# Softmax attention with a feed-forward branch on one core: another order of work in the opening and around five groups of pair sums

## The chip, the cores and the metric

The kernel runs on one core of a Trainium2 chip. The core has five engines that work side by side, each through its own list of instructions in order: TensorE (PE, matrix products), ScalarE (ACT, here mostly exponentials), VectorE (DVE), GpSimd (POOL) and SyncE (SP, which only issues transfers). They wait for one another through semaphores. Products land in PSUM, which has eight banks of 128 partitions x 512 float32; all else that is on the chip lies in SBUF. The metric is the device time of one execution in microseconds (us). The kernel before takes 664.33 us, the median of three runs (664.21 to 664.44).

## The reference

Input x has 2048 rows of 640. Attention has 32 heads of 20 columns and one key and value head for all of them. Two branches work on the same normalized rows and are added to x:

```
xn = layernorm(x)
q = (xn @ wq).reshape(2048, 32, 20);  k = xn @ wk;  v = xn @ wv
p = softmax(q @ k.T * 20**-0.5)              # 32 heads x 2048 x 2048
attn = (p @ v).reshape(2048, 640) @ wo
ffn = relu(xn @ w1 + b1)**2 @ w2 + b2        # 1536 hidden columns
out = x + attn + ffn
```

Most of the time goes into the 32 x 2048 x 2048 exponentials.

## The kernel before, in words

**Tiles.** A score tile is 128 keys x 512 queries of one head. A block is four heads and one of four chunks of 512 queries; there are 32 blocks and 16 key tiles, so 512 units of four tiles each. PE makes a tile by one product of 20 rows (kT times qT) into a PSUM bank; seven banks are shared by such tiles and other work, and the eighth collects probabilities times values of the current block.

**Two ways through the exponential.** 348 units go to ACT: the line L1328 takes two score tiles (128x1024) from two banks, writes their exponentials into two of 16 slots of the buffer PT, and PE multiplies them by the values (vx). The order of these exponentials is fixed. The other 164 units, called sets here, go past ACT. DVE evicts each of the four tiles of such a set in a scaled and shifted 16-bit integer form whose bits, read as bf16, stand near an exponential (L1551). Three copies of the set follow, each with another constant added to the integers: POOL makes most (L1571, or two copies by one instruction, L2121, a joint pass), DVE some (L1572). The four terms, summed with weights, come near the exponential. PE multiplies each term by the values (vx for two terms, vxs, the values with a weight, for the others).

**Pair sums.** Two terms with one weight can be added first, so that PE has one product less for each of four heads. For this POOL issues a transfer within SBUF that adds one term into the other (tx<-tx, L1588; both pairs of a set at once, L2119; L2047 is the same where it was put in later), or DVE adds them (L1593, L2048). The product of the summed term waits for the landing. Each term lies in one of 15 buffers (tx); a buffer is used anew when all that reads it is done. A sum overwrites its second term, so the first sum of a set must come behind a joint pass that reads that term.

**Opening.** Rows of x come in by eight transfers. For each of the first four tiles of 128 rows DVE or ACT makes the statistics, DVE the normalized rows (L822), PE five transposes (T0 to T3, L866), ACT or DVE the eviction (L871 on ACT), then PE the key rows (K0 to K3), the query rows of the first block (Q0_0 to Q0_3) and the values (V0_0 to V0_3). ACT evicts the four query pieces (L887) and then begins with the first exponential. Ahead of the transposes PE runs dummy products of a constant tile of ones (`ones`, L734, in buffer OR) with a tile of zeros (`zero`, L735): three at L861 and 15 at L905. They compute nothing that is used.

**What sets the order.** A planner inside the program walks through a model of the engines while the kernel is built: each step carries a modelled duration, a priority and due times, and tables of rules change them by stage. Then a table (PLAN) permutes each engine's list, and a second model (replay) settles the places of the buffers. So an instruction's place does not stand in the code by its line. L729 is a helper that records nearly all products, so its line says nothing of which product it is; the names of the tiles do.

Of the kernel before, what the change touches and what calls it, by code (L numbers as in the profile page):

```python
# [2257 lines left out]
```

## Time and profile before

| what | before |
|---|---|
| time, median of 3 runs | 664.33 us (664.21 to 664.44) |
| span of the profiled execution | 663.4 us |
| ACT busy | 649.3 us (98%), of it 640.3 us in 696 exponentials |
| PE busy | 655.2 us (99%), with modelled ends |
| DVE busy | 627.1 us (95%) |
| POOL busy | 533.1 us (80%) |
| joint passes on POOL (L2121) / single passes (L1571) | 16 / 369 |
| transfers that add a pair (512 KB) | 111, landing after 5.7 us (median) |

The profile gives no device time for the profiled execution alone, only its span, from its first instruction to its last; the median of the runs lies 0.9 us above that span. In the profile's rows a group has a count, the busy time in us, the mean length of one in ns, and the idle time ahead of it with the engine that ended it. Engines start an instruction before the last one has ended, so the busy time of a group is less than count times mean. PSUM buffers are called ps in the rows; PT, tx, kT and qT are as above, xnT is the transposed normalized rows, and names of form in_A_x_dram are inputs.

### The profile page before, as it was taken

Reading aid. Unit: us, or ns where it says so; the run is one execution under the profiler, and the core shown is the slowest. Engines: PE = TensorE matmul, PEld = TensorE weight load, DVE = VectorE, ACT = ScalarE, POOL = GpSimd, SP = SyncE. Lnnn points to the kernel's source line nnn. Section 1 sums busy time; section 2 is a strip of 40 time slices with the busy share of each in tenths; the row PEclk is TensorE's granted clock in tenths of the full one; section 3 lists DMA queues with packets and bytes.
Section 4 is the critical chain, followed back from the end, with each engine's and each line's share of the span. In section 5 each row is a group of like instructions: output and inputs, shape, how many; then the busy total and the mean of one; then the engine's idle time right before and its main releaser. Section 6 shows DMA issues by size and latency. Waiting matters only on the chain. (4 is left out here: it accounts for less than half of the span.)

```text
span 663.4 us, 22377 instructions
## 1 busy us (share of the span) xinstructions
PE 655.2 (99%) x9569; PEld 211.9 (32%) x9570; DVE 627.1 (95%) x1125; ACT 649.3 (98%) x719; POOL 533.1 (80%) x528
## 2 busy tenths in 40 slices
PE   8999999999999999999999999999999999999997
PEld 4432222332322223323332222333333322223444
DVE  8979999999999999999999999999999999999997
ACT  7999999999999999999999999999999999999995
POOL 1629899898998889898999988889899999799300
PEclk9999999999999999999999999999999999999999
DMA  8594957788997995696957645798788655858741
GB/s 289 160 241 109 197 119 161 163 183 189 190 191 162 185 179 117 127 182 125 181 105 154 126 91 102 154 180 176 151 170 167 131 126 97 172 104 182 136 111 70
DMA packets 53528, 102.09 MB, mean 154 GB/s; under 512 B 15916, under 2 KB 31164, under 8 KB 53364
## 3 DMA queue, kind: packets, MB, share of 16 engines
q0 software_dynamic: 18544, 68.17, 55.5%
q1 hardware_dynamic: 34164, 31.94, 16.6%
q8 instruction: 75, 1.23, 0.8%
q10 hardware_dynamic: 720, 0.54, 0.3%
q14 instruction: 25, 0.20, 0.1%
HBM read 23.26 MB, written 10.01 MB: 50 GB/s over the span
## 5 line engine op out<-in xcount | busy, mean ns | idle before, releaser
L1328 ACT ACTIVATE PT<-ps 128x1024 bf16<-128x1024 f32 x696 | 640.3, 1121 | 2.2 <-PE ps L729 1.7
L1551 DVE TENSOR_SCALAR tx<-ps 128x512 uint16<-128x512 f32 x656 | 424.0, 683 | 21.1 <-PE ps L729 14.2
L1571 POOL INT64_ADD tx<-tx x369 | 391.2, 1130 | 57.3 <-PE ps L729 16.8
L729 PE MATMUL ps<-qT,kT 20*128 20x512 bf16 x2048 | 262.9, 384 | 0.3
L729 PEld LDWEIGHTS ps<-qT,kT 20*128 20x128 bf16 x2048 | 67.3, 91 | 253.3 <-ACT PT L1328 132.9
L729 PE MATMUL ps<-PT,vx 128*32 128x512 bf16 x1392 | 131.3, 384 | 0.0
L729 PE MATMUL ps<-tx,vxs 128*32 128x512 bf16 x1220 | 112.9, 384 | 0.4 <-DMA tx<-tx 0.3
L1588 POOL DMA_DIRECT2D tx<-tx x103 | 102.8, 998 | 7.7 <-POOL tx L1571 6.9
L729 PE MATMUL ps<-w_sb,big 128*32 128x320 bf16 x1536 | 82.6, 302 | 0.0
L729 PE MATMUL ps<-tx,vx 128*32 128x512 bf16 x864 | 81.0, 384 | 1.6 <-DMA tx<-tx 1.6
L729 PE MATMUL ps<-xnT,w_sb 128*32 128x512 bf16 x960 | 78.9, 383 | 0.0
L1572 DVE TENSOR_SCALAR tx<-tx 128x2048 uint16<-128x2048 uint16 x91 | 63.3, 707 | 0.8 <-DMA tx<-tx 0.5
L729 PEld LDWEIGHTS ps<-PT,vx 128*32 128x32 bf16 x1392 | 34.3, 94 | 39.7 <-issue 35.2
L729 PEld LDWEIGHTS ps<-w_sb,big 128*32 128x32 bf16 x1536 | 34.0, 95 | 31.1 <-issue 20.3
L729 PEld LDWEIGHTS ps<-tx,vxs 128*32 128x32 bf16 x1220 | 28.5, 94 | 36.5 <-issue 27.6
L1054 DVE TENSOR_SCALAR hT_tmp<-ps,b1col 128x512 bf16<-128x512 f32 x48 | 35.7, 743 | 1.6 <-PE ps L729 1.3
L729 PE MATMUL ps<-xnT,wq_sb 128*32 128x512 bf16 (+2 forms) x480 | 35.6, 356 | 0.0
L729 PE MATMUL ps<-wo_c,OC 128*32 128x320 bf16 x576 | 31.8, 301 | 0.0
L2121 POOL INT64_ADD tx<-tx x16 | 30.6, 1913 | 0.5
L729 PEld LDWEIGHTS ps<-tx,vx 128*32 128x32 bf16 x864 | 20.9, 95 | 27.9 <-issue 20.5
L729 PEld LDWEIGHTS ps<-xnT,w_sb 128*32 128x32 bf16 x960 | 19.3, 94 | 25.7 <-issue 17.4
L1416 DVE COPY OR<-ps 128x512 f32<-128x512 f32 x30 | 20.5, 682 | 0.9 <-PE ps L729 0.6
(91 smaller groups left out, 242.6 us busy)
## 6 DMA issues: line engine op xcount, KB each, us to landing
tx<-tx POOLq DMA_DIRECT2D x111, 512.0 KB, 5.7
tx<-tx POOLq DMA_DIRECT2D x7, 1024.0 KB, 9.0
w_sb<-in_B_w_dram SPq DMA_DIRECT2D x8, 480.0 KB, 9.4
big<-OR SPq DMA_DIRECT2D x71, 40.0 KB
xb<-in_A_x_dram SPq DMA_DIRECT2D x1, 2560.0 KB, 12.2
xb<-b2r POOLq DMA_DIRECT2D x1, 2560.0 KB, 19.0
xr<-xb SPq DMA_DIRECT2D x16, 160.0 KB, 3.4
out_dram<-out_sb SPq DMA_DIRECT2D x15, 160.0 KB, 2.9
```

Source lines behind the costliest of these rows:

```text
L729: return lambda e: e.matmul(out_(), l, val(r), start=val(start), stop=val(stop), tile_position=tp, skip_group_check=loose)
L1054: o = Op(f"RL{qc}_{f}", "DVE", 0.66, [lambda e: e.tensor_scalar(out=hT_tmp[:, k % 2, :], in0=ps[:, at(bk), :], scalar1=b1col[:, f:f + 1], ...
L1328: o = Op(f"ACT{st_['j']}", "ACT", ACB + ACM * n, [lambda e: e.activation(out=PT[:, slots[0].n:slots[0].n + n, :], in_=src(), func=AF.Exp, ...
L1416: tn = op(f"TN{b}", "DVE", 0.60, lambda e: e.tensor_copy(out=OR[:, a, :], in_=ps[:, PVB, :]), [lastpv] + or_users[a], prio=0)
L1551: d1 = op(f"D1_{n}_{i}", "DVE", 0.60, lambda e: e.tensor_scalar(out=L()[:, cs].bitcast(U16), in0=ps[:, ref.n, :], scalar1=XA, scalar2=XB, ...
L1571: fns = dict(POOL=lambda e, T=T, j=j: e.int64_add(out=T().bitcast(I64), in0=L().bitcast(I64), in1=TSTEP * j * 0x0001000100010001), DVE=lam ...
L1572: DVE=lambda e, T=T, j=j: e.tensor_scalar(out=T().bitcast(U16), in0=L().bitcast(U16), scalar1=TSTEP * j, scalar2=None, op0=ALU.add))
L1588: p = op(f"AD{a}_{n}", "POOL", ADDUR, lambda e, src=src, dst=dst: e.dma_start(dst(), src(), accum_op=ALU.add), dp + [ad_last.get(k)], dma= ...
L2121: fn = lambda e, x=x: e.int64_add(out=two(*sorted((x["ref"][2].n, x["ref"][3].n))).bitcast(I64), in0=two(*sorted((x["ref"][0].n, x["ref"][ ...
```

## The change

The planner, its rules and the replay are taken out, and the order is written down: a table ORDER has the names of all steps of each engine in their order, with the banks or buffers that they take; TENANTS says which terms live in each of the 15 tx buffers, one behind the other; HELD says behind which DVE step a POOL step has to wait. The functions that make the steps are the same. Cut to its core:

```diff
-RULES = {0: {'WARM': 1},
...
-PLAN = {
-    "PE": (
-        "0*39 1 2 16 21 4 0 28 1*2 2 0 15 ...
...
+NSET = 15
...
+ORDER = {
+    "PE": (
+        "W4 W5 W6 warm: warm: warm: warm: warm: warm: warm: warm:S1a warm:S1b warm:S1b warm:AG1 warm:S3a warm:S3a T0 T1 T2 T3 K0 Q0_1 Q0_0 Q0_3 Q0_2 K1 K2 q:0,1,2@0,1,2 q:3,4@3,4 V0_0 V0_1 "
...
+TENANTS = (
+    ("108 119 172 246 319 298 368 446 426 507 ...
...
+        for e in ENG:
+            nth = {}
+            for word in ORDER[e].split():
...
+                if k in ("fill", "warm"):
...
+                else:
+                    nth[k] = nth.get(k, -1) + 1
+                    o = made[k if k in made else f"{k}.{nth[k]}"]
+                    o.banks = ns
+                    names[e].append(o.name)
```

Compared step by step, the order differs in five stretches, in the time of the kernel before: from the start to some 74 us (called A below), 147 to 168 us (B), 231 to 247 us (C), 280 to 301 us (D) and 452 to 494 us (E). Everywhere else each engine has the same steps one behind the other. Over the whole, 13 dummy products stand where 15 stood (the three ahead of them stay), two fills of zeros instead of 12, 693 exponentials instead of 696 (six in the opening take three tiles, 128x1536), 650 evictions of scores into sets instead of 656 (six take two tiles), 86 passes on DVE instead of 91, 360 single passes on POOL instead of 369, and 23 joint ones instead of 16.

The first place is the head of DVE's list. In both, L734 (now L603) is the tile of ones, hT_tmp the zeros, and PT, ident the steps that make the identity matrix for the transposes. Before:

```order
L734 MEMSET OR 128x128
L735 MEMSET hT_tmp 128x256
L736 MEMSET scr 128x4
L738 MEMSET PT 128x1
L739 MEMSET ident 128x64
L741 TENSOR_SCALAR PT<-PT 128x1
```

and now:

```order
L607 MEMSET PT 128x1
L610 TENSOR_SCALAR PT<-PT 128x1
L610 TENSOR_SCALAR PT<-PT 128x2
L610 TENSOR_SCALAR PT<-PT 128x4
L604 MEMSET hT_tmp 128x256
L610 TENSOR_SCALAR PT<-PT 128x8
L610 TENSOR_SCALAR PT<-PT 128x16
L611 STREAM_TRANSPOSE PT<-PT 128x32
L608 MEMSET ident 128x64
L612 TENSOR_SCALAR ident<-PT 32x32
L614 MEMSET vx 128x16
L616 MEMSET zeros 128x16
L605 MEMSET scr 128x4
L612 TENSOR_SCALAR ident<-PT 32x32
L615 MEMSET vx 128x16x11
L603 MEMSET OR 128x128
L612 TENSOR_SCALAR ident<-PT 32x32 x2
```

The tile of ones, which the first product of PE reads, has gone from the first to the sixteenth place of DVE's list; the steps ahead of it are the same ones as before, in another order.

The second place is the head of PE's list, up to the first scores (ps<-qT,kT). L861 and L905, now L709 and L1029, are the dummies; wk_c is K, wq_sb is Q0, wv_c is V0. Before:

```order
L861 MATMUL ps<-hT_tmp,OR 128x512 x3
L905 MATMUL ps<-hT_tmp,OR 128x512 x15
L866 MATMUL ps<-ident,big 128x128 x20
L729 MATMUL ps<-xnT,wk_c 20x128 x20
L729 MATMUL ps<-xnT,wq_sb 20x128 x60
L729 MATMUL ps<-xnT,wk_c 20x128 x20
L729 MATMUL ps<-xnT,wq_sb 20x128 x20
L729 MATMUL ps<-xnT,wk_c 20x128 x20
L890 MATMUL ps<-wv_c,xnT 128x20 x10
L729 MATMUL ps<-xnT,wk_c 20x128 x20
L729 MATMUL ps<-qT,kT 128x512 x4
```

and now:

```order
L709 MATMUL ps<-hT_tmp,OR 128x512 x3
L1029 MATMUL ps<-hT_tmp,OR 128x512 x13
L699 MATMUL ps<-ident,big 128x128 x20
L599 MATMUL ps<-xnT,wk_c 20x128 x20
L599 MATMUL ps<-xnT,wq_sb 20x128 x80
L599 MATMUL ps<-xnT,wk_c 20x128 x40
L599 MATMUL ps<-qT,kT 128x512 x5
L702 MATMUL ps<-wv_c,xnT 128x20 x10
L599 MATMUL ps<-xnT,wk_c 20x128 x20
```

All four query pieces now stand ahead of the second key tile, and the first five score tiles ahead of the values and the last key tile; the transposes stay behind all dummies.

The third place is POOL's list in stretch B, around the sets 106 to 109. L1571 (now L1094) is a single pass, L1588 (now L1118) the issue of a pair sum, L1100 a joint pass. Before:

```order
L1588 DMA tx<-tx 128x2048
L1571 ISA tx<-tx 128x1024 x5
L1588 DMA tx<-tx 128x2048
L1571 ISA tx<-tx 128x1024 x2
L1588 DMA tx<-tx 128x2048
```

and now:

```order
L1118 DMA tx<-tx 128x2048
L1100 ISA tx<-tx 128x2x1024
L1094 ISA tx<-tx 128x1024 x3
L1118 DMA tx<-tx 128x2048
L1100 ISA tx<-tx 128x2x1024
L1118 DMA tx<-tx 128x2048
L1094 ISA tx<-tx 128x1024 x3
```

The first three issues in each are the sums of the sets 108, 107 and 106, one behind the other. Ahead of set 107's stand one joint pass (set 109, copies 2 and 3) and three single ones instead of five; between set 107's and set 106's one joint pass (set 106) instead of two single ones.

Besides these, SP's loads stand in another order (the first part of wq behind the rows 8 to 11, the rest of wq behind b1), ACT issues wk behind its table load and wv behind the statistics, and POOL issues the transfer that adds b2 to x (xb<-b2r, L1153) behind its last normalized rows, just ahead of the library load that its passes need, instead of four rows earlier.

More of the change, by code (lines that the diff above doesn't have):

```diff
@@ new lines, in transposes, with v_mats @@
+        def transposes(st, bk):
+            return [(lambda e, dt=dt: e.transpose(out=psbf(bk)[:, dt * 128:(dt + 1) * 128], in_=xn_sb[:, st, dt:D:DT], identity=ident[:])) for dt in range(DT)]
+        def v_mats(st, bk):
+            return [(lambda e, dt=dt: e.matmul(ps[:, at(bk), DH * (st % 4):DH * (st % 4) + DH], xnT[:, dt, st * 128:(st + 1) * 128], wv_c[:, dt, :], start=(dt == 0), stop=(dt == DT - 1)))
+                    for dt in range(DT)]
+        VB0, WB = SHARED[2], 7
+        k_of, q_of, v_of, vs_of, first_rel = {}, {b: [] for b in range(NBLK)}, {}, {}, {}
@@ L907, in need_te, with evac @@
+        def evac(ref, *args, **kw):
+            o = op(*args, **kw)
+            o.gives = [ref]
+            return o
         def need_te(sts):
             return [te_op[st] for st in sts]
[L910 to L921 removed]
@@ new lines, in bass_parallel_sum__grouped_kv_mqa__dense_activation_squared_relu__prompt_kernel @@
+        for b in range(NBLK):
+            pv_all[b][-1].ends[1] = True
+            made[f"TN{b}"].deps += pv_all[b]
+        seq = {e: [made[w] for w in names[e]] for e in ENG}
+        assert sum(map(len, seq.values())) == len(made), [w for w in made if w not in sum(names.values(), [])]
+        for o in made.values():
+            o.deps = [made[d] if isinstance(d, str) else d for d in o.deps]
+        same = {}
+        for o in made.values():
+            if o.dma is not None:
+                same.setdefault((id(o.dma), o.tgt[1]), []).append(o)
@@ new lines, in bass_parallel_sum__grouped_kv_mqa__dense_activation_squared_relu__prompt_kernel @@
+        slot_rel = {}
+        pv_tile = {HPG * o.unit + h: o for l in pv_all for o in l if o.unit is not None for h in range(HPG)}
+        for o in seq["ACT"]:
+            for n, t in zip(o.slots, o.tiles):
+                if n in slot_rel:
+                    o.deps.append(slot_rel[n])
+                slot_rel[n] = pv_tile[t]
+        made[f"OFe{ST - 1}_0"].deps += [slot_rel[n] for n in (0, 1)]
+        made[f"OFe{ST - 1}_1"].deps += [slot_rel[n] for n in (0, 1)]
+        filler = {(u, j): o for e in ("DVE", "POOL") for o in seq[e] for u, j in o.fills}
@@ new lines, in bass_parallel_sum__grouped_kv_mqa__dense_activation_squared_relu__prompt_kernel @@
+        for n, tenants in enumerate(TENANTS):
+            free_after = list(xn_op.values()) if n >= NMORE else []
+            for k in map(int, tenants.split()):
+                u, j = divmod(k, NTERM)
+                assert sets[u].at[j] == n
+                filler.pop((u, j)).deps += free_after
+                free_after = sets[u].reads[j]
+        assert not filler
+        held = iter(HELD.split())
+        for o in seq["POOL"]:
+            if o.lock:
+                w = next(held)
+                if w != "-":
+                    o.deps.append(made[w])
```

1988 lines of the change are left out of this document (406 added, 1582 removed), and 444 rows, old and new, of tables (HELD, ORDER, PLAN, TENANTS).

## The prediction

> **What bounds the kernel now.** I read the page first, then the ACT rows of the timeline, then the waits.
>
> ```profile
> span 663.4 us, 22377 instructions
> PE 655.2 (99%) x9569; PEld 211.9 (32%) x9570; DVE 627.1 (95%) x1125; ACT 649.3 (98%) x719; POOL 533.1 (80%) x528
> L1328 ACT ACTIVATE PT<-ps 128x1024 bf16<-128x1024 f32 x696 | 640.3, 1121 | 2.2 <-PE ps L729 1.7
> ```
>
> Three engines read 95% or more, and PE's ends are modelled, so shares don't decide. The timeline of ACT from 11 us on does:
>
> ```profile
> 12.18 152.27 ACT L1328 ACTIVATE PT<-ps 128x1024 bf16<-128x1024 f32 x165 [0.23 <-PE ps L729]
> 165.09 299.03 ACT L1328 ACTIVATE PT<-ps 128x1024 bf16<-128x1024 f32 x325 [0.64 <-PE ps L729]
> 464.60 36.87 ACT L1328 ACTIVATE PT<-ps 128x1024 bf16<-128x1024 f32 x40 [0.48 <-PE ps L729]
> ...
> 556.93 97.55 ACT L1328 ACTIVATE PT<-ps 128x1024 bf16<-128x1024 f32 x106 [0.18 <-PE ps L729]
> ```
>
> From 12.18 us to 556.93 + 97.55 = 654.48 us ACT does exponentials with hardly a pause, so the span has three parts: the start of the first exponential, 696 pitches (the time from one start to the next), and a tail of 663.4 - 654.5 = 8.9 us whose order is unchanged. The span shrinks only by an earlier start, fewer exponentials, or shorter pitches. Hidden stalls lie inside the busy time, since each exponential starts before the last has ended; they show as a longer pitch. The groups by stretch give it as (busy + idle - mean) / (count - 1):
>
> ```profile
> L1328 ACT ACTIVATE PT<-ps 128x1024 bf16<-128x1024 f32 x23 | 21.4, 1038 | 0.3 <-PE ps L729 0.2
> L1328 ACT ACTIVATE PT<-ps 128x1024 bf16<-128x1024 f32 x45 | 41.7, 1086 | 0.2
> L1328 ACT ACTIVATE PT<-ps 128x1024 bf16<-128x1024 f32 x80 | 73.5, 1165 | 0.0
> L1328 ACT ACTIVATE PT<-ps 128x1024 bf16<-128x1024 f32 x24 | 22.5, 1111 | 0.6 <-PE ps L729 0.6
> L1328 ACT ACTIVATE PT<-ps 128x1024 bf16<-128x1024 f32 x19 | 17.9, 1115 | 0.0
> L1328 ACT ACTIVATE PT<-ps 128x1024 bf16<-128x1024 f32 x24 | 22.3, 1051 | 0.0
> L1328 ACT ACTIVATE PT<-ps 128x1024 bf16<-128x1024 f32 x47 | 43.5, 1084 | 0.5 <-PE ps L729 0.5
> ```
>
> These are 12 to 33 us and 33 to 74 (A), 74 to 146.6 (unchanged order, my yardstick), then B, C, D and E. The yardstick's pitch is (73.5 - 1.165) / 79 = 0.916 us. A's two halves have 0.926 (the start's wait left out) and 0.928, B 0.956, C 0.932, D 0.924, E 0.933. Above the yardstick that is 22 x 0.010 + 44 x 0.012 = 0.75 us in A, and 23 x 0.040 = 0.93, 18 x 0.017 = 0.30, 23 x 0.008 = 0.19, 46 x 0.017 = 0.80 in B to E, together 2.2. The excess is what an altered order can give back there.
>
> What stands behind it in B to E, from the waits and PE's timeline:
>
> ```profile
> PE ps L729 <- DMA tx<-tx: 1.9, 4, 0.6
> 164.29 0.40 PE L729 MATMUL ps<-tx,vx 128*32 128x512 bf16 x4 [0.64 <-DMA tx<-tx]
> 239.71 0.40 PE L729 MATMUL ps<-tx,vx 128*32 128x512 bf16 x4 [0.31 <-DMA tx<-tx]
> 292.17 0.40 PE L729 MATMUL ps<-tx,vxs 128*32 128x512 bf16 x4 [0.31 <-DMA tx<-tx]
> 463.80 0.40 PE L729 MATMUL ps<-tx,vx 128*32 128x512 bf16 x4 [0.62 <-DMA tx<-tx]
> ```
>
> PE stands still four times in the whole program for a pair sum that has not landed, once in each of B to E. Its list is in order, so the score products behind wait too, and the exponential that needs them: ACT's 0.64 at 165.09 and 0.48 at 464.60 follow.
>
> **Part 1, the start of the exponentials: +0.4 us.** The first product of PE reads the tile of ones.
>
> ```profile
> 0.82 0.17 DVE L734 MEMSET OR<- 128x128 bf16 x1 [0.82 <-PEq L2243]
> 2.58 0.97 DVE L743 TENSOR_SCALAR ident<-PT 32x32 bf16<-32x32 f32 x4
> 3.94 0.49 DVE L806 BATCH_NORM_STATS2 OR<-tx 128x6 f32<-128x320 bf16 x1
> 1.32 1.46 PE L861 MATMUL ps<-hT_tmp,OR 128*128 128x512 bf16 x3 [1.32 <-DVE PT L738]
> 7.58 1.44 PE L866 MATMUL ps<-ident,big 128*128 128x128 bf16 x20
> L905 PE MATMUL ps<-hT_tmp,OR x9: 464/631/631, 2.6 to 6.0; 128*128 128x512 bf16 x9
> L905 PE MATMUL ps<-hT_tmp,OR x8: 379/379/631, 5.6 to 7.4; 128*128 128x512 bf16 x8
> ```
>
> All constants are made when the first statistics begin at 3.94 us. With `ones` in sixteenth place the two last comparisons (2 x 0.24) stand behind it, so it is done by about 3.4 and PE begins 2.1 us later than at 1.32. The last two rows (queried before and after 6.1 us) show the dummies' durations fall from 631 to 379 ns near 6 us. Their pitch up to there is 3.4 / 8 = 0.43 us; behind it 0.24, from the weight loads of the same group, six in 1.2 us. The summary row reads "PEclk 9" for this time, so I take the change from the durations. The same sum for before: (6.15 - 1.32) / 0.43 = 11.2 dummies at 0.43 us, 6.8 at 0.24, an end at 7.8 where the transposes began at 7.58. For after, if the speed changes at the same time: 6.4 at 0.43, 9.6 at 0.24, an end at 8.45, less the same 0.2: 8.25, or 0.7 us late. Two dummies fewer save 2 x 0.24 of what would have been 1.2.
>
> Not all of it reaches the first exponential. Ahead of it ACT waited 0.23 us (above) and 0.28:
>
> ```profile
> 10.86 0.28 ACT L887 ACTIVATE qT<-ps 128x128 bf16<-128x128 f32 x1 [0.28 <-PE ps L729]
> 9.97 0.61 ACT L887 ACTIVATE qT<-ps 128x128 bf16<-128x128 f32 x3
> 9.23 1.01 PE L729 MATMUL ps<-xnT,wq_sb 128*20 128x128 bf16 x60
> 11.74 0.39 PE L729 MATMUL ps<-qT,kT 20*128 20x512 bf16 x4
> ```
>
> The fourth query piece now stands ahead of K1, the scores ahead of V0 and K3. If both waits vanish, 0.7 - 0.5 = +0.2 is left, if none, +0.7; I take +0.4. The floor is 0, because ACT's own chain behind the transposes keeps its rows; the ceiling comes with rival 1.
>
> The moved loads I cost at nothing: the first part of wq is issued two transfers later, but its first product stands at 9.23 us and moves back with the transposes; if it lands late all the same, the ceiling below holds that too. The rest of wq is needed only by block 1. POOL's moved transfer puts off the library load behind it:
>
> ```profile
> 28.58 1.81 POOL L1153 DMA_DIRECT2D xb<-b2r  x1
> 47.03 1.04 POOL L1571 INT64_ADD tx<-tx  x1 [12.09 <-PE ps L729]
> 48.71 3.07 POOL L1571 INT64_ADD tx<-tx  x3 [0.63 <-DVE tx L1551]
> 52.83 2.05 POOL L1571 INT64_ADD tx<-tx  x2 [1.06 <-DVE big L1062]
> ```
>
> The 12.09 us ahead of POOL's first pass is mostly that load. It moves by up to 1.8; the waits of 0.63 and 1.06 behind it cover 1.7, and DVE has passes there too. Uncovered, it would cost the first sets a product, a few tenths.
>
> **Part 2, three exponentials fewer: -0.2 us.** Nine pairs of tiles become six triples. The trace has no triple. Three query evictions of 128 columns, in the row at 9.97 above, have a pitch of (0.61 - 0.28) / 2 = 0.165 us; a line through that and the pairs' 0.916 gives 0.06 us for an instruction without columns, and 0.165 itself bounds it from above. Three instructions fewer save 0.18 to 0.5, or nothing where a triple waits for its third bank. I take 0.2, by the nearer rows.
>
> **Part 3, pitches in A: -0.3 us.** The bounds are 0 and 0.75. Ten fills of zeros (four products each) leave PE,
>
> ```profile
> L729 PE MATMUL ps<-kT,zeros 128*32 128x512 bf16 x48 | 4.5, 382 | 0.0
> ```
>
> and 40 of these 48 at that group's rate are 3.8 us of PE, most of it beside ACT. I take less than half of the bound, since A's pitch never held ACT for long.
>
> **Part 4, B to E: -1.6 us.** In B the late sum is that of set 106:
>
> ```profile
> 153.10 0.90 POOL L1588 DMA_DIRECT2D tx<-tx  x1
> 154.03 1.05 POOL L1571 INT64_ADD tx<-tx  x1
> 155.77 1.04 POOL L1571 INT64_ADD tx<-tx  x1 [0.68 <-DVE OC L1452]
> 156.75 0.86 POOL L1588 DMA_DIRECT2D tx<-tx  x1
> L2121 POOL INT64_ADD tx<-tx x16 | 30.6, 1913 | 0.5
> ```
>
> Before, two passes and 0.68 of waiting lie between the two issues. After, one joint pass (1.91, from L2121) does: the issue of 106 comes at about 153.10 - 0.2 (one joint and three single passes ahead instead of five single) + 0.9 + 1.95 = 155.75, 1.0 us earlier. The wait was 0.64, so the product finds its sum, if the transfer takes no longer. C to E have the same kind of edit around waits of 0.31, 0.31 and 0.62. The bounds are 0 (or a loss, rival 2) and the 2.2 us of excess; the four waits are 1.9. I take 1.6, allowing that one short wait stays. Six fewer evictions and five fewer passes on DVE lie beside ACT's work: nothing.
>
> **The sum.** +0.4 - 0.2 - 0.3 - 1.6 = -1.7 us. The page's span of 663.4 becomes 661.7; the median lies 0.9 above the span, so 664.3 becomes 662.6 us. The bounds' ends are -3.45 (0, -0.5, -0.75, -2.2) and, with rival 1's start, +2.1.
>
> **Rivals.** Rival 1: the change of the dummies' speed comes later, because PE starts later. If it depends on how long PE has been busy, the 4.8 us between 1.32 and 6.15 repeat from 3.4, and it comes at 8.2. The 16 dummies then take 11.2 pitches of 0.43 us and 4.8 of 0.24, to 9.35, less 0.2: transposes at 9.15, 1.6 late; if it comes later still, all 16 take 0.43, to 10.2, 2.4 late. So 1.6 to 2.4, about 2.0 for the first exponential less a few tenths of the vanished waits: +1.7 for +0.4, and 662.6 becomes 663.9. For it: the row of 631 ns lasts as far as 6 us and nothing in this trace shows why it ends there. Against it: if a fixed beat sets it, 2.7 us of work up to 6.15 may be enough. The Trainium skill ("TensorE: Matmul & The Clock Gate", Part 1) says that the clock opens after a busy window of about 3.4 us which runs freely and does not start with the kernel, and that the point varies from run to run. By that rule the later start risks a whole window more, and the time would scatter; the trace, with one opening near 6 us, agrees but can't show the phase. Chance 0.25.
>
> Rival 2, slower: the joint passes make new late sums. A joint pass takes 1.91 where a single copy takes 1.05, and the set's first sum must stand behind it. Where the product has less than 0.9 us of margin, PE waits as it did at 164.29. Four waits of 0.64 with none of the old excess regained give +0.4 - 0.2 - 0.3 + 2.6 = +2.5: 666.8. It decides from about 0.5 us per stretch on. For it: four late sums among 111 show margins near nothing. Against it: in B the issue comes earlier by its rows. Chance 0.11.
>
> Rival 3: the regained waits come back one product later, since the excess pitch is a shortage of PE or DVE in these stretches and not the sum's lateness; only the opening changes, -0.1 or so: 664.2. For it: C and D show excess without any idle time of ACT. Against it: E's and B's excess is about as large as their waits on PE. Chance 0.14.
>
> **How the numbers follow.** The forecast, 662.6 us, has 0.50; its own range is 661.3 to 663.7. Faster or slower by over 0.2% (1.3 us, about what a measurement of this kernel can tell from no change) means under 663.0 or over 665.7. Of the forecast 0.41 lies below 663.0 and 0.09 above; of rival 1, 0.04 below and 0.21 between; rival 3 is the same; rival 2 is slower. So faster 0.45, same 0.44, slower 0.11. The range of 8 in 10 reaches from 661.2 to 665.2: it holds the forecast's range and rivals 1 and 3, and leaves out rival 2.
>
> **What would show it.** Part 1: the first dummy near 3.4 us, the first transpose near 8.25 and the first exponential near 12.6 in ACT's timeline; a first transpose after 9 us is rival 1. Part 2: a triple with a pitch under 1.37 (one and a half pairs). Parts 3 and 4: pitches in B to E near 0.916 (0.93 leaves half), and no PE wait on tx<-tx above 0.3 us; several waits of 0.6 are rival 2, no waits but unchanged pitches rival 3. The forecast is wrong if the exponentials begin after 13.5 us, or if the stretch from the first to the last of them is not shorter by 1.5 us or more.

## The result, and the profile after

The changed kernel takes 672.0 us, the median of four runs (668.92 to 676.69), against 664.38 us before (664.21 to 665.63): 1.0114 times the time before, 95% interval 1.0078 to 1.0149. It is slower by 1.1%, and its runs scatter over 8 us where those before scatter over 1.4. Six more runs of it gave 667.97 to 677.60. The granted clock belongs to the result: it reads under 0.999 in nine of these ten runs, down to 0.984, while of 112 runs of the kernel before, timed beside the experiments, seven did so, none under 0.995. Here and below a ratio and its interval leave out single runs that lie more than 1.5% above the fastest of their kernel; the ranges in brackets hold them.

First the span and the row of the exponentials from the page of the profiled execution, and the exponentials on ACT down to their last pause of over 0.2 us (start, time from there to the next pause, the first instruction's form, the count, and in brackets the wait ahead). L1071 is what L1328 was, L599 what L729 was.

```profile
span 669.3 us, 22210 instructions
L1071 ACT ACTIVATE PT<-ps 128x1024 bf16<-128x1024 f32 (+1 forms) x693 | 640.3, 1123 | 6.9 <-PE ps L599 6.4
12.45 72.39 ACT L1071 ACTIVATE PT<-ps 128x1536 bf16<-128x1536 f32 x76
85.81 85.73 ACT L1071 ACTIVATE PT<-ps 128x1024 bf16<-128x1024 f32 x93 [0.97 <-PE ps L599]
173.11 1.02 ACT L1071 ACTIVATE PT<-ps 128x1024 bf16<-128x1024 f32 x1 [1.57 <-PE ps L599]
175.08 1.02 ACT L1071 ACTIVATE PT<-ps 128x1024 bf16<-128x1024 f32 x1 [0.95 <-PE ps L599]
176.56 1.02 ACT L1071 ACTIVATE PT<-ps 128x1024 bf16<-128x1024 f32 x1 [0.46 <-PE ps L599]
177.79 67.02 ACT L1071 ACTIVATE PT<-ps 128x1024 bf16<-128x1024 f32 x73 [0.21 <-PE ps L599]
246.29 70.01 ACT L1071 ACTIVATE PT<-ps 128x1024 bf16<-128x1024 f32 x76 [1.48 <-PE ps L599]
316.75 189.98 ACT L1071 ACTIVATE PT<-ps 128x1024 bf16<-128x1024 f32 x206 [0.46 <-PE ps L599]
```

The pauses of 0.64 and 0.48 us at 165 and 464 us have gone. In their place stand 0.97 at 85 us, 3.2 in four pieces at 172 to 178, 1.48 at 246 and 0.46 at 316. ACT's list has the same order in both kernels, so the start of one and the same exponential can be subtracted. The difference, after less before, at exponentials named by their start in the kernel before:

| start before (us) | 12.2 | 23.3 | 83.5 | 101.9 | 157.0 | 168.7 | 179.7 | 240.1 | 246.0 | 301.4 | 312.5 | 644.1 |
|---|---|---|---|---|---|---|---|---|---|---|---|---|
| after less before (us) | +0.27 | -0.07 | -0.69 | +0.54 | +0.71 | -0.17 | +3.55 | +3.64 | +4.96 | +4.58 | +5.20 | +5.23 |

The opening gains 0.96 us from the first exponential to 83 us, B 0.88 up to 169 us; between 84 and 102, 169 and 180, 240 and 246 and 301 and 312 us the kernel gives back 1.23, 3.72, 1.32 and 0.62. From 312 us on the sum does not change. Stretch E brought nothing in the end, though the wait for its pair sum has gone: the exponentials gain 0.64 us there (from +5.40 at 460 us to +4.76 at 465) and have lost it again by 490 (+5.39). PE waits for an eviction instead:

```profile
471.87 0.39 PE L599 MATMUL ps<-qT,kT 20*128 20x512 bf16 x4 [0.38 <-DVE tx L1081]
```

The rest of the 5.9 us of span, 0.7, lies behind the last exponential.

What PE, and in one case DVE, waited for at these four places, as the timelines of the two engines show it:

```profile
84.83 0.40 PE L599 MATMUL ps<-tx,vx 128*32 128x512 bf16 x4 [1.05 <-DMA tx<-tx]
170.68 0.69 DVE L971 TENSOR_TENSOR OC<-cmore 128x512 bf16<-128x512 f32 x1 [2.52 <-DMA cmore<-drs]
172.03 0.38 PE L599 MATMUL ps<-qT,kT 20*128 20x512 bf16 x1 [1.65 <-DVE tx L1081]
245.31 0.40 PE L599 MATMUL ps<-tx,vx 128*32 128x512 bf16 x4 [1.58 <-DMA tx<-tx]
315.78 0.62 PE L599 MATMUL ps<-tx,vx 128*32 128x512 bf16 x8 [0.54 <-DMA tx<-tx]
```

Three are pair sums. The one at 172 us, the dearest, goes back to another transfer: the reciprocals of the softmax sums, sent through DRAM and spread over the rows (cmore<-drs), for which the product L971 on DVE (CM0_2) waits. DVE stood still for 2.52 us, so the eviction behind it came late, so PE stood still for 1.65 us for the bank.

Then the clock closed. The windows view of PE (window, its length, busy time, instructions, the granted clock, DMA share, GB/s):

```profile
167.00:170.50 3.50, 3.38 (x59) 1.00 0.85 187
170.50:173.90 3.40, 1.87 (x21) 0.98 0.82 198
173.90:177.30 3.40, 3.40 (x31) 0.52 0.64 146
177.30:180.70 3.40, 3.40 (x53) 1.00 0.68 137
```

In the 3.4 us behind the standstill PE ran at half its clock and got 31 instructions through, against 53 in the next 3.4 us; that is where the waits of 0.95 and 0.46 come from.

How long the transfer took, by SP's timeline. Issued first are the reciprocals (drs<-R, called RS4), then, when they have landed, the two transfers that bring them back (cmore<-drs, BC4_0 and BC4_3). Before:

```profile
152.79 0.63 SPq L1423 DMA_DIRECT2D drs<-R  x1
157.77 1.42 SPq L1445 DMA_DIRECT2D cmore<-drs  x2
159.23 0.85 SPq L1420 DMA_DIRECT2D R<-drs  x1
```

and after:

```profile
153.00 0.57 SPq L943 DMA_DIRECT2D drs<-R  x1
160.95 0.77 SPq L964 DMA_DIRECT2D cmore<-drs  x1
163.00 0.87 SPq L941 DMA_DIRECT2D R<-drs  x1
163.91 0.62 SPq L964 DMA_DIRECT2D cmore<-drs  x1
```

Two things are late: the way out, from the issue of RS4 to that of BC4_0, took 7.95 us instead of 4.98, and BC4_3 now stands behind a load of x (XR2) and R<-drs (SL5) on SP's list, 2.96 us behind BC4_0, where it followed BC4_0 directly.

### The profile page after: what moved, and what is told of

Its sections match the earlier page's. It is cut to its first block, busy times and chain, and to the rows that moved or that the text cites. A ratio compares the mean times of both kernels' runs of the same rounds, so it can differ in the third digit from the quotient of the medians.

```text
span 669.3 us, 22210 instructions
## 1 busy us (share of the span) xinstructions
PE 655.2 (98%) x9525; PEld 212.7 (32%) x9526; DVE 622.9 (93%) x1114; ACT 649.2 (97%) x716; POOL 536.5 (80%) x526
## 3 DMA queue, kind: packets, MB, share of 16 engines
q8 instruction: 75, 1.23, 0.8%
## 4 chain that ended last, share of the span: by engine, by line
PE 81%; DMA 7%; POOL 6%; ACT 2%; DVE 1%; issue 1%; SPq 0%; POOLq 0%
PE ps L599 80%; DMA tx<-tx 5%; POOL tx L1094 4%; ACT PT L1071 2%; POOL tx L1118 1%; DMA drs<-R 1%; DMA cmore<-drs 1%; POOL tx L1100 1%; DVE tx L1081 1%; PE ps L1029 1%; PE ps L699 0%; PE ps L709 0%; SPq L868 0%; PE ps L702 0%; DVE PT L1007 0%
## 5 line engine op out<-in xcount | busy, mean ns | idle before, releaser
L1071 ACT ACTIVATE PT<-ps 128x1024 bf16<-128x1024 f32 (+1 forms) x693 | 640.3, 1123 | 6.9 <-PE ps L599 6.4
L1081 DVE TENSOR_SCALAR tx<-ps 128x512 uint16<-128x512 f32 (+1 forms) x650 | 423.5, 688 | 27.6 <-PE ps L599 21.0
L1094 POOL INT64_ADD tx<-tx x360 | 384.6, 1163 | 56.9 <-DVE tx L1095 23.8
L599 PE MATMUL ps<-qT,kT 20*128 20x512 bf16 x2048 | 266.2, 385 | 3.1 <-DVE tx L1081 2.0
L599 PEld LDWEIGHTS ps<-qT,kT 20*128 20x128 bf16 x2048 | 68.4, 91 | 255.6 <-ACT PT L1071 133.7
L599 PE MATMUL ps<-PT,vx 128*32 128x512 bf16 x1392 | 131.8, 386 | 0.0
L1118 POOL DMA_DIRECT2D tx<-tx x118 | 120.3, 1032 | 10.9 <-POOL tx L1094 6.9
L599 PE MATMUL ps<-tx,vxs 128*32 128x512 bf16 x1220 | 112.4, 385 | 0.0
L599 PE MATMUL ps<-tx,vx 128*32 128x512 bf16 x864 | 81.5, 385 | 3.2 <-DMA tx<-tx 3.2
L599 PE MATMUL ps<-w_sb,big 128*32 128x320 bf16 x1536 | 80.3, 302 | 0.0
L599 PE MATMUL ps<-xnT,w_sb 128*32 128x512 bf16 x960 | 78.1, 383 | 0.0
L1095 DVE TENSOR_SCALAR tx<-tx 128x2048 uint16<-128x2048 uint16 x86 | 60.0, 712 | 0.2
L599 PEld LDWEIGHTS ps<-PT,vx 128*32 128x32 bf16 x1392 | 34.3, 94 | 42.0 <-issue 36.5
L1100 POOL INT64_ADD tx<-tx x23 | 45.2, 1966 | 1.5 <-DVE tx L1095 0.8
L599 PEld LDWEIGHTS ps<-w_sb,big 128*32 128x32 bf16 x1536 | 33.6, 95 | 30.0 <-issue 19.6
L599 PEld LDWEIGHTS ps<-tx,vxs 128*32 128x32 bf16 x1220 | 28.3, 94 | 34.6 <-issue 27.5
L827 DVE TENSOR_SCALAR hT_tmp<-ps,b1col 128x512 bf16<-128x512 f32 x48 | 35.6, 742 | 2.4 <-PE ps L599 2.1
L599 PE MATMUL ps<-xnT,wq_sb 128*32 128x512 bf16 (+2 forms) x480 | 34.4, 356 | 0.0
L599 PE MATMUL ps<-wo_c,OC 128*32 128x320 bf16 x576 | 31.5, 301 | 0.0
L599 PEld LDWEIGHTS ps<-tx,vx 128*32 128x32 bf16 x864 | 20.9, 95 | 29.9 <-issue 20.7
L599 PEld LDWEIGHTS ps<-xnT,w_sb 128*32 128x32 bf16 x960 | 19.0, 94 | 26.8 <-issue 18.6
L939 DVE COPY OR<-ps 128x512 f32<-128x512 f32 x30 | 20.5, 683 | 0.8 <-PE ps L599 0.5
```

Source lines behind the costliest of these rows:

```text
L599: return lambda e: e.matmul(out_(), l, val(r), start=val(start), stop=val(stop), tile_position=tp, skip_group_check=loose)
L827: o = evac(ref, f"RL{qc}_{f}", "DVE", lambda e: e.tensor_scalar(out=hT_tmp[:, k % 2, :], in0=ps[:, ref.n, :], scalar1=b1col[:, f:f + 1], s ...
L939: tn = evac(pv_ref[b], f"TN{b}", "DVE", lambda e: e.tensor_copy(out=OR[:, a, :], in_=acc()), or_users[a])
L1071: o = op(f"a:{a}", e, lambda e, qk=qk, slots=slots: e.activation(out=some(PT, slots), in_=some(ps, [r.n for r in qk.takes]), func=AF.Exp, ...
L1081: o = op(f"e:{a}", e, lambda e, x=x, i=i, n=n, refs=refs: e.tensor_scalar(out=x.ref(0)[:, i * 512:(i + n) * 512].bitcast(U16) if n == 1 el ...
L1094: fn = dict(POOL=lambda e, x=x, j=j: e.int64_add(out=x.ref(j).bitcast(I64), in0=x.ref(0).bitcast(I64), in1=TSTEP * j * 0x0001000100010001) ...
```

## The experiments

Each edit is made in the written order; words like BC4_3 are steps, and a line with - or + shows where a word stood and stands. The line numbers of the edited kernels are 20 or 21 higher (L1091 for L1071, L619 for L599). "At full clock" below means a granted clock of 0.999 or 1.000 over the run.

**e1: the late transfer at 171 us.**

```diff
 SP:
-RS4 BC4_0 XR2 SL5 BC4_3 FW28
+RS4 BC4_0 BC4_3 XR2 SL5 FW28
```

> One edit to the changed kernel: on SP the transfer BC4_3 (cmore<-drs, the reciprocals' broadcast that the DVE product CM0_2 waits for) is issued ahead of XR2 and SL5 instead of behind them, some 2 us earlier. Theory W (late transfers hold the queues, and the clock drop at 174 us follows from PE's stall there): CM0_2's wait of 2.52 us falls under 0.6, the exponentials between 160 and 183 us lose under 1 us instead of 3.7, no clock drop at 174 us, time 667 to 669 with little scatter. Theory R (the slow part is the reciprocals' way out, RS4 to BC4_0, 7.9 us instead of 5.0, and the issue place of BC4_3 does not matter): the wait stays above 1.5 us and the time stays near 670 to 672.

Measured: 667.25 us (665.93 to 676.96, six runs), ratio 1.0034 (1.0014 to 1.0053); four of six runs at full clock. In its profile CM0_2 does not wait, and the exponentials at 180 us come 0.67 us earlier than before the change instead of 3.55 later. SP's timeline says how much of it is the edit's:

```profile
152.66 0.58 SPq L963 DMA_DIRECT2D drs<-R  x1
157.66 1.73 SPq L984 DMA_DIRECT2D cmore<-drs  x2
```

The way out took 5.0 us here, without being touched; BC4_3 stands behind it in SP's list and cannot have hurried it. So both theories hold a part. Over all executions without this edit the way out took 7.95, 7.8, 10.7 and 7.8 us with waits of 2.5 to 2.9 on CM0_2 (the changed kernel twice, e5, e8), and 5.2 and 5.0 us with waits of 0.8 (e2, e3). With the edit it took 4.6 to 6.5 us in eight executions and CM0_2 waited in one of them alone (e12, 2.49 us, where RS4 itself was issued 4.5 us later). Why the way out is long in four of the six executions without the edit and in none of the eight with it was not found.

**e2: keep PE busy in the standstill.**

```diff
 PE:
+fill fill fill fill fill fill fill fill
 d:143.1
```

> One edit to the changed kernel: eight products of zeros are put on PE ahead of the score product d:143.1, where PE stood still for 1.65 us at 172 us; they need nothing and add zeros. Theory G (the half-speed stretch at 174 to 177 us is the clock's answer to that standstill, and the scatter of 668.9 to 676.7 comes from it): the wait on CM0_2 stays, PE keeps busy, the clock reads 1.000 in every run, and the time is 668 to 669.5 with a scatter under 1 us. Theory O (the clock drops come from elsewhere, from the opening's phase for instance): times from 669 to 677 as before, with clocks under 1.000 in most runs.

Measured: 668.49 us (667.33 to 668.86, four runs), ratio 1.0054 (1.0041 to 1.0067), all four at full clock. The median is theory G's number, but the runs scatter over 1.5 us and not under 1. And in the one execution with a profile CM0_2 waited only 0.81 us, and the exponential at 172.5 us waited mostly for the dummies themselves:

```profile
172.52 69.98 ACT L1092 ACTIVATE PT<-ps 128x1024 bf16<-128x1024 f32 x76 [1.69 <-PE ps L620]
```

So four of four runs at full clock against one of ten speak for G; this profile alone does not show a long wait without a closing clock. What does speak beside it: in all five profiled executions with a wait of 2.49 us or more on CM0_2 (after twice, e5, e8, e12) the clock closed next, for one or two stretches of 3.4 us, and in none of the others did it close there.

**e3 and e4: the pair sums' waits.**

```diff
 SP:
-SL1 wo3 QD4_3 OM1_2 RS1
+SL1 QD4_3 OM1_2 wo3 RS1
 PE:
-u:171.1 v:169 q:704,705 d:189.3 FFN0_10 u:172.2 q:706,707 d:188.1 v:170 FFN0_10 u:172.1
+v:169 q:704,705 d:189.3 FFN0_10 u:172.2 q:706,707 d:188.1 v:170 FFN0_10 u:171.1 u:172.1
-u:236.1 u:238.1 q:920,921 d:254.3 d:252.0 u:237.1 q:922,923
+u:238.1 q:920,921 d:254.3 d:252.0 u:237.1 u:236.1 q:922,923
```

> Three edits to the changed kernel, none at the 171 us stall: on SP the load wo3 goes behind OM1_2 (3 us later, away from the sum s:44.0 issued 0.2 us ahead of it), on PE the product u:171.1 goes behind six further pieces (about 2 us later), and u:236.1 behind one pair of scores, one sum product and one set score (0.5 us later). Theory W: the waits of 1.05 (85 us), 1.58 (245 us) and 0.54 us (316 us) go, the exponentials come 2.5 to 3 us earlier, the clock drop near 174 us stays possible: 666 to 669 where the clock reads 1.000 or 0.997, more where it is lower. Theory S (PE, DVE or POOL are short there and the waits come back one step later): less than 1 us gained, 669 to 672.

> All edits of e1 and e3 together. Theory W: what the opening gained (0.8 us by 45 us) and what B to E were to give stays, without the four stalls: clock 1.000 in all runs and 661.5 to 663.5, under the kernel before. Theory S: 665 to 668, since removed waits return elsewhere. Theory O (clock drops unbound to these stalls): a scatter of several us stays.

Measured: e3 668.2 us (664.71 to 674.04, ten runs, five of them with a clock of 0.986 to 0.992), ratio 1.0062 (1.0031 to 1.0094); e4 665.11 us (663.78 to 683.93, twelve runs), ratio 1.0008 (0.9997 to 1.0018). The waits at 85, 245 and 316 us are gone in both profiles, and did not return one step later (in e7 below, which has the same edits, 0.99 us stand at 314.6 us again). e4's exponentials:

```profile
13.68 400.03 ACT L1091 ACTIVATE PT<-ps 128x1536 bf16<-128x1536 f32 x433
413.91 52.70 ACT L1091 ACTIVATE PT<-ps 128x1024 bf16<-128x1024 f32 x57 [0.20 <-PE ps L619]
466.95 34.27 ACT L1091 ACTIVATE PT<-ps 128x1024 bf16<-128x1024 f32 x37 [0.34 <-PE ps L619]
```

400 us without a pause, as the order was meant to run. From its first to its last exponential e4 needs 1.8 us less than the kernel before in its first profile (0.8 less than in its second, b1 below), and begins 1.5 us later: no gain is left. At 85 us e1, e2, e5 and e8 had no wait either, with wo3 in its old place, so what made the sum s:44.0 late in the changed kernel's executions is not shown; the wait at 245 us stood in every execution without its edit (1.2 to 1.8 us). The run at 683.93 had a clock of 0.970; the cause did not lie in the four places alone.

**e5 and e6: the late start.**

```diff
 DVE:
-idr id1 id2 id4 zero id8 ... vx0 ones ide0
+ones zero idr id1 id2 id4 id8 ... vx0 ide0
```

> One edit to the changed kernel: the tile of zeros and the tile of ones are made first on DVE again; 16 dummy products as in the changed kernel. Theory P (the opening's start is set by when the dummies begin and by the clock's phase against it): the first dummy at 1.2 to 1.4 us, the first transpose at 7.4 to 8.0 and the first exponential at 11.7 to 12.3, where the executions with the ones in sixteenth place had 12.45 to 13.86; the stalls at 172 and 245 us stay, so 666 to 671. Theory Q (the opening is bound by the rows' loads and statistics, the dummies don't matter): the first exponential stays at 12.4 or later.

> e4 with the tiles of zeros and ones made first. Theory P: e4 began its exponentials at 13.68 and had 1.8 us less than the kernel before between the first and the last one; with a start at 12.0 the span is 662.0 to 662.8 and the time of undisturbed runs 663 to 663.8, 1 us under the kernel before. Theory Q, or new stalls because the exponentials come 1.6 us earlier against transfers that do not: 664.5 to 666 as e4.

> The kernel before once more, to see whether its opening has the same spread. Theory P: its 18 dummies begin at 1.32 us, so the clock opens between 4 and 7.6 us, the first transpose comes at 7.4 to 8.3 and the first exponential at 11.9 to 12.9, a spread under 1 us. A first exponential above 13 us would speak against it.

Measured: e5 667.99 us (666.11 to 676.64), ratio 1.0037 (1.0023 to 1.0052), with the stalls at 172 and 245 us; e6 663.49 us (662.52 to 672.53, twelve runs), ratio 0.9989 (0.9980 to 0.9999). The kernel before began its exponentials at 12.18 us again, and its time was 664.39 us with a span of 662.6. The first transpose came at 7.60 or 7.61 us in all seven executions with the ones first, and at 8.40, 8.89, 8.92, 9.18, 9.24, 9.64 and 9.82 in the seven with the ones in sixteenth place, whose first exponentials lay between 12.45 and 13.86, 13.2 in the mean. PE's timeline of the changed kernel, and then of e3, the latest of them, shows why:

```profile
3.46 1.46 PE L709 MATMUL ps<-hT_tmp,OR 128*128 128x512 bf16 x3 [3.46 <-DVE OR L603]
4.72 3.85 PE L1029 MATMUL ps<-hT_tmp,OR 128*128 128x512 bf16 x13
8.40 1.28 PE L699 MATMUL ps<-ident,big 128*128 128x128 bf16 x20
```

```profile
3.47 1.46 PE L729 MATMUL ps<-hT_tmp,OR 128*128 128x512 bf16 x3 [3.47 <-DVE OR L623]
4.72 5.26 PE L1049 MATMUL ps<-hT_tmp,OR 128*128 128x512 bf16 x13
9.82 1.28 PE L719 MATMUL ps<-ident,big 128*128 128x128 bf16 x20
```

The dummies start at 3.46 or 3.47 us each time and take 3.85 us in the one execution and 5.26 in the other; the moment at which the clock opens and their pitch falls from 0.43 to 0.22 us lay between 6.5 and 9.4 us. In two executions of the kernel before it lay at 6.15 and 4.05 us, and the first transpose at 7.58 and 7.48, since there the normalized rows come last and not the dummies. For the transposes theory P holds and Q falls. For the first exponential P is half the story: in the five executions with the ones first and the changed order on PE it came at 11.89, 11.95, 12.37, 12.48 and 12.84 us, three of them later than P's 12.3. There the next limit is the first part of wq, issued two transfers later than before. It lands at 9.4 to 10.4 us, where it landed at 6.0 to 6.8 in the three profiles of the old order (e9 included); the first query product starts 0.13 or 0.14 us behind its landing in all five, and the first exponential 2.3 us behind that. The transfer in the kernel before and in e11, with its size and the time to its landing, and PE's row in e11:

```profile
wq_sb<-in_A_wq_dram SPq DMA_DIRECT2D x1, 100.0 KB, 5.1
wq_sb<-in_A_wq_dram SPq DMA_DIRECT2D x1, 100.0 KB, 7.4
10.16 1.30 PE L619 MATMUL ps<-xnT,wq_sb 128*20 128x128 bf16 x80 [0.62 <-DMA wq_sb<-in_A_wq_dram]
```

e6 has a lower median than both kernels, by 0.1% against the kernel before, at the edge of what these runs tell apart, and it is not sound: its profiled execution had a span of 670.7 us. The windows view of PE for it:

```profile
9.00:12.30 3.30, 2.71 (x146) 1.00 1.11 386
12.30:15.70 3.40, 3.27 (x58) 0.93 1.05 386
15.70:19.10 3.40, 3.20 (x33) 0.50 0.69 239
19.10:39.60 20.50, 20.50 (x217) 0.51 0.29 84
39.60:43.00 3.40, 3.40 (x56) 1.00 0.56 158
```

Here the clock closed in the opening, though PE stood nowhere for long, and stayed at half for 24 us; the exponentials are 0.19 us late at the first and 7.87 us at the one of 35.6 us. This is a second way to lose, apart from the stall at 172 us.

**e7, e8 and e9: the dummies that were dropped.**

```diff
 PE:
-V0_3 q:5,6,7
+V0_3 warm: warm: q:5,6,7
-v:0 q:13,14
+v:0 fill q:13,14
... (a fill each behind KT2, v:2, v:1, T9, v:9, v:10, d:27.0, v:13, two behind T7)
```

The kernel before has 17 dummies of the group that counts 13 in the changed one, 15 ahead of the transposes and two more at 13 to 14 us; e7 and e8 put back those two. e9 is the kernel before with its fills narrowed:

```diff
-mm(lambda jj=jj: ps[32 * jj:32 * jj + 32, PVB, :], zeros32[:, :], kT[:, 0:512], ...)
+mm(lambda jj=jj: ps[32 * jj:32 * jj + 32, PVB, 0:8], zeros32[:, :], kT[:, 0:8], ...)
```

> e6 with the dummies of the opening that the change had dropped put back near their old places: two of ones and ten of zeros between 13 and 45 us. Theory F (these dummies hold the clock open through the opening's thin stretch, and the runs at 0.98 to 0.985 are those in which it closed there for several 3.4 us stretches, as e6's profile shows from 15.7 to 39.6 us): no run under 0.995, no run above 666, typical time 663.0 to 664. Theory N (the dummies do not matter to the clock): again one run in ten near 672, and 0.3 to 1.5 us lost because PE has more to do.

> The changed kernel with only those twelve dummies put back. Theory F: the runs near 672 to 677 with clocks of 0.985 to 0.995 become rare (a drop of one 3.4 us stretch at 172 us stays possible, clock 0.997): times 666.5 to 671. Theory N: the spread of 668 to 677 stays.

> The kernel before with its twelve products of zeros (four instructions each) cut from 512 to 8 columns, so that the order stays and PE's work in them is nearly gone; nothing of the result depends on them. Theory F: some runs fall to a clock of 0.98 to 0.995 and 668 to 675, where the 43 executions of the kernel before that were timed here beside mine had two above 665.8; the others stay at 664 to 664.6. Theory N: all runs at 664 to 665.5 as before.

Measured: e7 665.98 us (665.12 to 672.61, eleven runs), ratio 1.0025 (1.0007 to 1.0044); e8 670.14 us (667.01 to 672.65, six runs), ratio 1.0076 (1.0051 to 1.0101); e9 663.77 us (663.13 to 664.98, eleven runs, all at full clock), ratio 0.9988 (0.9980 to 0.9997). Theory F falls: the kernel before keeps its clock without the fills' work, and e7 lost its clock in two of eleven runs with them. They cost time instead. e8 gains nothing in the opening: its exponentials are 1.10 us late at the first and 2.19 us late at 83 us, where the changed kernel without the dummies had gone from +0.27 to -0.69. The thirteen dummies (two of ones and eleven of zeros, one more than the change had dropped; the expectation counts ten) cost 2.0 us there, and ACT's timeline of e8 shows waits that the changed kernel did not have:

```profile
21.03 15.17 ACT L1092 ACTIVATE PT<-ps 128x1536 bf16<-128x1536 f32 x15 [0.77 <-PE ps L620]
36.43 4.69 ACT L1092 ACTIVATE PT<-ps 128x1024 bf16<-128x1024 f32 x5 [0.22 <-PE ps L620]
41.41 43.57 ACT L1092 ACTIVATE PT<-ps 128x1024 bf16<-128x1024 f32 x47 [0.29 <-PE ps L620]
```

In the kernel before, the work in the fills costs 0.1%: in e9 the exponential of 83 us comes 0.57 us earlier. e9 has a lower median than the kernel before, like e6, and unlike e6 it kept its clock in all its runs.

**e10: the other cure at 245 us.** Against e6; on PE u:171.1 is back in the changed kernel's place.

```diff
 POOL:
-j:172.2 b:172.3 p:171.1 s:171.0 p:171.2
+j:172.2 p:171.1 s:171.0 b:172.3 p:171.2
```

> e6 with another cure at 245 us: the product u:171.1 stays in the changed kernel's place, and on POOL the pass p:171.1 and the sum s:171.0 go ahead of the transfer b:172.3, which adds both pairs of set 172 (1 MB) and whose first product comes 14 us later. Theory W (the sum was late because it was issued 3 us behind a transfer twice as large): the sum is issued 2 us earlier with nothing large ahead of it, no wait at u:171.1, exponentials at 245 us as in e6, 662.5 to 664 in undisturbed runs. Theory S (the sum's own 7.6 us from issue to product are too few there): the wait of 1 us or more stays at u:171.1, 664.5 to 666.

Measured: 667.92 us (665.12 to 679.63, twelve runs), ratio 1.0053 (1.0033 to 1.0074), ten clocks under 0.999. My expectation was wrong: the wait did not go, it moved to the transfer now issued second and grew to 2.26 us:

```profile
232.80 2.10 POOL L1138 DMA_DIRECT2D tx<-tx  x2 [0.30 <-POOL tx L1114]
243.97 0.40 PE L619 MATMUL ps<-tx,vxs 128*32 128x512 bf16 x4 [2.26 <-DMA tx<-tx]
```

I had overlooked that set 172's other product, u:172.2, stands at 241.7 us, not 14 us behind. From the first issue to the last landing the two transfers took 11.2 us here and 12.3 in the changed kernel (233.01 to the end of the wait at 245.31). So in these two orders the 1.5 MB took 11 to 12 us, and the product of the second one stood too early for that in both; exchanging the two on POOL's list only moves the wait.

**e11, e12 and e13: the clock in the opening.**

```diff
 SP (e11, e13):
-X12 xb b1 wq w10
+X12 wq xb b1 w10
 PE (e12, e13):
-K0 Q0_1 Q0_0 Q0_3 Q0_2 K1 K2 q:0,1,2 q:3,4 V0_0 V0_1 K3 V0_2 V0_3
+K0 Q0_0 Q0_1 Q0_3 K1 Q0_2 K2 V0_0 V0_1 K3 q:0,1,2 q:3,4 V0_2 V0_3 warm: warm:
```

> e6 with the order of SP's loads behind X12 as in the kernel before: the rest of wq, then the 2.5 MB copy xb, then b1. Theory X (the copy, issued first, crowds the loads and instruction fetches on which PE waits in the opening): no run with a clock under 0.995, typical time 663 to 664. Theory Y (the new order of PE's products leaves the array thin between 11 and 16 us): about one run in five still under 0.995, up to 672.

> e6 with the opening's products on PE in the order of the kernel before, from K0 to the first scores (the values V0_0, V0_1 and K3 ahead of the scores again), and two dummies of ones behind V0_3. Theory Y: no run under 0.995, the first exponential up to 0.5 us later, 663.3 to 664.3. Theory X: one run in five still under 0.995.

> e11 and e12 together. Either theory: no run under 0.995, 663.3 to 664.5. If runs near 670 remain here as well, neither the copy's place nor this order of products is the cause, and it stays open.

Measured: e11 664.01 us (663.45 to 668.50, eleven runs), ratio 0.9998 (0.9983 to 1.0013), lowest clock 0.995; e12 665.98 us (663.98 to 674.91, twelve runs), ratio 1.0026 (1.0007 to 1.0044), seven clocks under 0.999; e13 666.5 us (664.16 to 682.35, twelve runs), ratio 1.0045 (1.0014 to 1.0076), six. The old order of the products on PE does not cure it; theory Y falls. e11 by itself would fit theory X, but e13, for which both theories said that no run would lie under 0.995, has the same edit on SP and five clocks from 0.972 to 0.984, so X is not shown either. Why the clock closes in the opening of some executions stays open.

**The changed kernel once more.**

> The changed kernel once more, for its spread: by the executions so far its first exponential comes between 12.4 and 13.9 us, the stalls at 172 and 245 us stand in every execution, the one at 85 us in some, and the time is 667 to 677 with a clock of 1.000 in under half the runs.

Measured: 670.44 us (667.97 to 677.60, six runs), ratio 1.0100 (1.0056 to 1.0144), no run at full clock. Its profile has the waits of the first one again, 0.77 at 86 us, 1.62 at 173, 1.61 at 248 and 0.35 at 319 us, and the clock closed behind the second for two stretches instead of one.

## Why the prediction was wrong

- **What bounds the kernel** was right: the exponentials' start, their pitches and the tail carry the whole difference. Of the 5.9 us more span, 5.2 lie there.
- **Part 1 (+0.4 us)** had the mechanism right and the size wrong. The dummies began at 3.46 us, as worked out (3.4), and the first profile fits the sum (first transpose 8.40 for 8.25, first exponential 12.45 for 12.6). That fit is luck: I took the moment of the speed's change from one execution as given, and in this profile it came at 6.5 us, the earliest of seven. Over the seven executions the first exponential came 0.3 to 1.7 us later than before, 1.0 in the mean; rival 1 (+1.7) is the upper end of this scatter and not another case. The loads that were put at nothing cost nothing here: the first query product comes behind the landing of wq (9.93 and 9.52 us), and POOL's first pass comes 1.4 us later (48.41 for 47.03) while the exponentials gain. The late wq matters only once the dummies start early (e5, e6, e7, e10, e11).
- **Part 2 (-0.2)** fits: from start to start a triple takes 1.33 us and a pair behind one 0.904, so six triples take 0.15 us less than nine pairs. **Part 3 (-0.3)** was too small: with part 2 the gain is 0.96 us up to 83 us, the same in the changed kernel and in e1 and e4 to within 0.01. The dropped dummies, which I put mostly beside ACT, are worth 2.0 us on the path in the changed order by e8, and by e9 the work in the fills is worth 0.57 in the old one. What I treated as a small term of the change was its best one.
- **Part 4 (-1.6 us)** is the step that failed: "the product finds its sum, if the transfer takes no longer". In place of -1.6 us, the exponentials lost 5.9 from 83 us on. I moved the issue by the rows and kept the landing at the old interval. In stretch B the sum's wait did go (0.88 us gained up to 169 us). But the step had looked at pair sums alone, and at the altered stretches alone: the waits at 85 and 316 us stand where every engine has its old order, and no term of the sum could hold them. At 172 us the edit had moved SP's transfers, and the reciprocals came back 2.5 us too late for their product. I had this list of moved transfers for the opening and left it out for B. In C the sum of set 171 was put 3 us behind one of 1 MB and landed 9.1 us after its issue where 7.6 were left. With the waits cured (e4), B, C and D bring 0.7, 0.3 and 0.4 us against the first profile of before, but 0.2 are lost between B's gain and C's, and 0.5 behind 312 us: 0.8 us net from 102 us to the last exponentials, half of what I forecast. In E the wait went and its 0.64 us came back within 25 us, which is rival 3 (chance 0.14) in that stretch. And the bound itself came from one recording: in its second profile (b1) the kernel before has only two of the four waits for pair sums, 0.9 us for 1.9, since those of C and E are missing, and its exponentials come 0.97 us earlier at the end; against that profile e4 gained nothing in B to E.
- **Rival 2** had the right sign and the nearest mechanism (new late transfers, +2.5 us, 666.8). I gave it 0.11 and left it outside the range. The waits it priced at 0.64 each were 1.05, 1.65, 1.58 and 0.54 on PE; by the table the four stretches cost 6.9 us, and some 1.6 us of that is the clock (the waits of 0.95, 0.46 and 0.21 at 175 to 178 us), which no case of mine had beyond the opening.
- **The sum's base** was off by 0.9 us: the run with this profile lies 1.8 us above its span (671.16 and 669.3), as does the kernel before in its second profile (664.39 and 662.6). If the first profile of before lies as far above its span, it was of an execution slower than the median. A difference of spans is not touched by it.

The Trainium skill ("TensorE: Matmul & The Clock Gate", Part 1) was right against my trust in one phase: it says that the window runs freely and that the number of products at low speed varies from run to run, and the 6.5 to 9.4 us above agree. On closing, the same page (its part on oscillation) names idle gaps of over 3.4 us; here standstills of 1.62 to 2.04 us at 172 us were enough five times out of five, while standstills of 1.2 to 2.3 us at 245 us closed it once in seven executions. The measurement decides. The busy time of PE in a stretch does not tell the two apart. In each trace the clock changes at whole multiples of 3.413 us from its first opening; of the changed kernel's stretches on that grid, these two hold its longest standstills, and the clock closed behind the first and stayed open behind the second:

```profile
170.33:173.74 3.41, 1.76 (x19) 1.00 0.78 186
242.01:245.42 3.41, 1.83 (x32) 1.00 0.90 170
```

In its second execution it closed behind a stretch with 2.36 us busy. What sets the threshold stays open.

## What to carry to other kernels

In a kernel that keeps several engines near their limit, a list of moved instructions is also a list of moved transfers: before trusting an earlier issue, list every transfer that the edit shifts on each queue, and give each consumer the time that the transfers issued within one landing take together. A margin taken from one recording is not a margin; here the same transfer needed 5 us in one execution and 8 to 11 in others. Where one late wait can close PE's clock, the price of that wait is two to three times its length (1.6 to 2.0 us of standstill, 3.7 to 5.2 us lost in five executions).

## What the runs showed of the hardware that I had not expected

- Pair sums do not run side by side for free: 512 KB land after 5.7 us and 1 MB after 9.0 in the median of the kernel before, 0.5 and 1 MB issued within 3.2 us of each other after 11 to 12 us, whichever goes first.
- The clock closes on 3.4 us stretches and can stay closed while PE's rows look full: 24 us at half speed in e6, of which the last 20.5 show PE busy without a gap, and 7.7 us lost between the first exponential and 36 us. In e6, e7, e10 and e12 it closed three stretches after it had first opened.
- One standstill of PE had no cause that the profile shows: 3.90 us ahead of a dummy that waits for nothing, in e7:

```profile
18.18 0.59 PE L1050 MATMUL ps<-hT_tmp,OR 128*128 128x512 bf16 x1 [3.90 <-issue]
```

- An exponential of three tiles is no bargain: in the changed kernel the six are busy for 9.0 us, and at 1.33 us from start to start each saves 0.025 against one and a half pairs.

```profile
L1071 ACT ACTIVATE PT<-ps 128x1536 bf16<-128x1536 f32 x6 | 9.0, 1495 | 0.0
```
